# Ranks between the two halves of the turn of x's rows, and the rows' transfers behind the ranks

## The chip, the cores and the metric

The kernel runs on one core of a Trainium2 chip. A core has five engines with instruction streams of their own: TensorE (PE in the profile, its weight loads PEld), VectorE (DVE), ScalarE (ACT), GpSimd (POOL) and SyncE (SP), which here only issues DMA transfers. They meet at semaphores. The metric is the device time of one execution in microseconds, as the median of several runs.

## The reference

A retention layer (linear attention with a decay per head) and, on its output, a mixture of experts with one expert for each token. B = 4 sequences of S = 768 tokens, H = 8 heads of D = 64, so 3072 tokens of 512 numbers; 8 experts with a hidden layer of 1024.

```python
# retention, for every head h with its decay gamma[h]
for t in range(S):
    state = gamma * state + outer(k[:, :, t], v[:, :, t])
    y[:, :, t] = scale * q[:, :, t] @ state
x = y.transpose(0, 2, 1, 3).reshape(B * S, H * D)
# the mixture: each token goes to the expert of its highest logit
xn = x / (norm(x) + 1e-6)
en = expert_emb / (norm(expert_emb) + 1e-6)
probs = softmax(xn @ en.T / tau)
e = argmax(probs, axis=1)
out = probs[e] * (relu(x @ w1[e]) @ w2[e])
```

## The kernel before

**Stages.** The retention runs first, then the eight experts, with some overlap at the seam. The retention is cut into blocks of 256 tokens, NM = 12 in all, three to a sequence. Its output, x, is written to a scratch tensor in DRAM (`xd`). Each token is given a slot in a table (`tbl`), sorted by expert, and the experts then gather their tokens' rows of x through that table. Expert 0 starts early, on the 288 of its slots that are filled first.

**Order.** The whole order is written out by hand: within an engine, instructions run in the order in which the program issues them, and the same holds for the transfers that SyncE issues. So where a line stands in the loop decides what waits behind it.

**One iteration m of the retention loop** (L754 to L882). `scores` makes 32 products of k and q into four PSUM banks (L374), and `masks` multiplies them on VectorE with the causal mask (L394), two banks for each half u of the block. `inter` (L444) adds the part of the carried state, and `state` (L408) makes the next block's. `logits_products` (L481) makes the router's logits of block m-1, `logits_rows` turns them on VectorE (L489). Then k and q of block m+1 are transposed (L343, L361) and copied by ScalarE. At the end of the iteration `intra` (L449) multiplies masked scores with v, and `take` (L451) copies the block's output from PSUM to `yTs[m]`.

**Rows of x.** `yTs[m]` has features on the partitions, and `xd` wants tokens as rows. `rows_turn(m)` (L458) turns the block with two VectorE transposes in blocks of 32 by 32, one for each half u of 128 tokens, from `yTs[m]` into a tile `x`. `rows(m)` (L465) then issues four transfers of that tile to `xd` on SyncE (L468). It is called for block m-1 near the end of iteration m (L853), ahead of `intra`. Three buffers hold `yTs`, two hold `x`.

**Slots.** The blocks are routed in groups: GROUPS = (0,1,2), (3,4,5), (6,7), (8), (9,10), (11). In the iteration after the last block of a group (`done`, L756), `sums` and `choose` pick each token's expert, and `add_counts` adds the group to the running counts. At the start of the next iteration (`waiting`, L757) `count` makes the ranks' sums on TensorE (L526 to L530), and `ranks` computes from them on VectorE rank and slot of each token (three instructions, `rs` L546, `rank` L548, `sloti` L550). `place` (L559) writes tokens into the table with indirect transfers on GpSimd, two to four for an iteration. `done` is set at m = 3, 6, 8, 9 and 11, so the ranks are computed at the start of m = 4, 7, 9 and 10; at m = 11 they come in the same iteration, in another branch.

**PSUM banks.** `pt_` hands out four banks (b0 to b3) in turn. In an iteration that starts with ranks, the first bank goes to the counts, the next four requests to the scores, then come the logits and the transposes. So the second half of the scores needs the bank that `rs` has read, and the logits and the transposes need banks that the masks have read.

**GpSimd.** `scale_k` and `scale_q` (L337, L332) of block m+2 wait for the first mask of iteration m; behind them stand the table writes of that iteration.

**The seam to the experts.** At the end of m = 8 two pieces of expert 0's weights are loaded (`load_piece`, L881, eight transfers at L191). At m = 9 and 10 `early_slots` reads table entries back on SyncE (L597), and at m = 10 `early_gather` fetches their rows from `xd` on GpSimd (L588, three transfers into `xge`). Two more pieces are loaded between the slot reads of m = 10. The rows of block 9 are written behind the last early gather (`gathered`). At m = 11 TensorE transposes `xge` (L607).

Of the kernel before, what the change touches and what calls it, by code (L numbers as in the profile page):

```python
# [11 lines left out]
F32 = mybir.dt.float32  # L12
# [12 lines left out]
P = 128  # L25
# [3 lines left out]
NM = B * NCB  # L29
# [5 lines left out]
KT = DM // P  # L35
FT = DF // P
Q = 32
NQ = P // Q
# [66 lines left out]
def retention_moe(ctx: ExitStack, tc: tile.TileContext, q, k, v, emb, tau, w1, w2, const, const16, out):  # L105
# [52 lines left out]
    def pt_():  # L158
        npt[0] += 1
        return bank(turn_of[npt[0] % len(turn_of)])  # L160
# [12 lines left out]
    def after(i, o):  # L173
        tc.add_manual_dep(i.ins, o.ins.name, SYNC, reason="pace")
# [135 lines left out]
    ap_ = ctxa.enter_context(tc.tile_pool(name="ap", bufs=2))  # L310
# [14 lines left out]
    def load_v(m, h=slice(0, H)):  # L325
        return load(vin[m % 4], v, m, h)
# [23 lines left out]
    def transpose_k(m, s, copy=nc.scalar.copy):  # L350
        ps = pt_()
        turn_k(m, s, ps)
        return copy_k(m, s, ps, copy)
# [43 lines left out]
    def state(m):  # L397

        if m % NCB == 0:
            for u in range(2):  # L400
                pst[u] = bank(f"pst{u}").rearrange("p (j c) -> p j c", j=KT)
        for j in range(KT):
            for sk in range(2):
                for u in range(1 + (m % NCB < NCB - 1)):
                    for a in range(2):
                        r = slice(u * 64, (u + 1) * 64)
                        h = 2 * j + a
                        i = nc.tensor.matmul(pst[u][a * D:(a + 1) * D, j, :D], ks_r[r, m % 3, sk, h, :], vin[m % 4][r, h, sk, :],  # L408
                                         start=(m % NCB == 0 and j == 0 and sk == 0), stop=True, skip_group_check=True)
        return i  # L410

    def state_copy(m):
        if m % NCB < NCB - 1:
            tBs[m] = ap_.tile([P, KT, D], F32, name="tB")
            nc.scalar.copy(out=tBs[m], in_=pst[1][:, :, :D])

    def state_sums(m):

        s1 = Ss[m, 1] = ap_.tile([P, KT, D], F32, name="s1")
        if m % NCB:  # L420
            nc.vector.tensor_tensor(out=s1, in0=pst[0][:, :, :D], in1=tBs[m - 1], op=ALU.add)
        else:
            nc.vector.tensor_copy(out=s1, in_=pst[0][:, :, :D])
        if m % NCB < NCB - 1:
            s0 = Ss[m + 1, 0] = ap_.tile([P, KT, D], F32, name="s0")
            nc.vector.tensor_tensor(out=s0, in0=pst[0][:, :, :D], in1=tBs[m], op=ALU.add)
# [3 lines left out]
    def py_of(m):  # L430
        pys[m] = [bank(f"py{u}").rearrange("p (j c) -> p j c", j=KT) for u in range(2)]
# [14 lines left out]
    def intra(m, u):  # L446
        for j in range(KT):
            for a in range(2):
                y_product(m, u, j, a, vs[m][:, u, 2 * j + a], pms[a, u][:, j])  # L449
# [5 lines left out]

            nc.scalar.copy(out=yTs[m][o * D:(o + 1) * D, :, P:], in_=pys[m][1][(1 - o) * D:(2 - o) * D])

    def rows_turn(m):  # L458
        x = ap_.tile([P, 2 * NQ, KT, Q], F32, name="x")
        for u in range(2):  # L460
            nc.vector.transpose(out=x[:, u * NQ:(u + 1) * NQ].rearrange("p g j a -> p j g a"),
                                in_=yTs[m][:, :, u * P:(u + 1) * P].rearrange("p j (g b) -> p j g b", b=Q))
        return x

    def rows(m, behind=None, x=None):  # L465
        x = rows_turn(m) if x is None else x
        for i in range(NQ):
            o = nc.sync.dma_start(  # L468
                out=xd[m * T2:(m + 1) * T2, i * P:(i + 1) * P].rearrange("(b g) x -> b g x", b=Q),
                in_=x[i * Q:(i + 1) * Q].rearrange("b g j a -> b g (j a)"))  # L470
            if behind is not None:
                after(o, behind)
# [19 lines left out]
    def span(g):  # L492
        return slice(2 * GROUPS[g][0], 2 * GROUPS[g][-1] + 2)
# [28 lines left out]
    def count(g):  # L522
        r = span(g)
        nb = r.stop - r.start
        pr = pt_()
        nc.tensor.matmul(pr[:, :nb * NE], ones, cum[:, r.start:r.start + 1].broadcast_to([P, nb, NE]), start=True,  # L526
                         stop=False, skip_group_check=True)
        nc.tensor.matmul(pr[:, :nb * NE], tri, oh[:, r], start=False, stop=False, skip_group_check=True)
        for i in range(1, nb):
            nc.tensor.matmul(pr[:, i * NE:nb * NE], ones, oh[:, r.start:r.stop - i], start=False, stop=(i == nb - 1),  # L530
                             skip_group_check=True)
        return pr
# [9 lines left out]
    def ranks(g, pr):  # L542
        r = span(g)
        nb = r.stop - r.start
        rs = ap_.tile([P, nb, NE], F32, name="rs", bufs=1)
        nc.vector.tensor_tensor(out=rs, in0=pr[:, :nb * NE].rearrange("p (c e) -> p c e", e=NE), in1=oh[:, r], op=ALU.mult)  # L546
        yield
        nc.vector.tensor_reduce(out=rank[:, r], in_=rs, axis=AX.X, op=ALU.add)  # L548
        yield
        nc.vector.scalar_tensor_tensor(out=sloti[:, r], in0=wmn[:, r], scalar=16.0 * STRIDE, in1=rank[:, r],  # L550
                                       op0=ALU.mult, op1=ALU.add)
        yield
# [13 lines left out]
    def run_all(*gs):  # L566
        gs = list(gs)
        while gs:
            gs = [g for g in gs if next(g, gs) is not gs]
# [29 lines left out]
    def early_gather(j):  # L599
        n = EROWS[j][1]  # L600
        indices(n, 0, slice(j, j + 1))
        return gather(xge, n, j, 0, j, SEALS[j] * P)
# [151 lines left out]
    for m in range(NM):  # L754
        nxt = m + 1 < NM
        done = last_of.get(m - 1)  # L756
        if waiting is not None:  # L757
            run_all(ranks(waiting, count(waiting)))
            ready += range(span(waiting).start, span(waiting).stop)
        py_of(m)  # L760

# [26 lines left out]
        if m == NM - 2:  # L788
# [5 lines left out]
            gathered = early_gather(2)  # L794
# [7 lines left out]
        if m == 0:  # L802
            state(0)
            state_copy(0)
            state_sums(0)
            intra(0, 0)
            intra(0, 1)
            transpose_k(1, 0)
            i = transpose_k(1, 1)
            after(load_v(2), i)  # L810
            inter(0)
            transpose_q(1, 0)
            i = transpose_q(1, 1)
            for j in (*load_q(3), load_k(3), load_v(3)):
                after(j, i)
            state(1)
            state_copy(1)
            state_sums(1)
        else:
            inter(m)  # L820
            if nxt:
                i = state(m + 1)
                state_copy(m + 1)
                if m + 3 < NM:
                    after(load_k(m + 3), i)
            if m == 2:
                after(nc.sync.dma_start(
                    out=tbl.rearrange("(e s) c -> e (s c)", e=NE)[:, :FILL * SW].rearrange("e (p x) -> e p x", p=P // NE),
                    in_=none), i)
            for i in () if m < 3 else (0, 1, 2) if m == 3 else (m - 1,):  # L830
                logits_rows(i, logits_products(i))
            if m == NM - 5:
                pad(0)
            if m == NM - 3:
                pad(1)
            if not nxt:
                pad(2)
            if nxt:
                state_sums(m + 1)
                spread_v(m, 1, nc.vector.tensor_copy)  # L840
                transpose_k(m + 1, 0)
                transpose_q(m + 1, 0)
                i = transpose_q(m + 1, 1)
                if m + 3 < NM:
                    after(load_v(m + 3), i)
                transpose_k(m + 1, 1)
                if done is not None:
                    z = sums(done)
                    run_all(choose(done, z))
                    run_all(add_counts(done))  # L850
                if m == NM - 2:
                    lows[1]()
                rows(m - 1, gathered if m == NM - 2 else None)  # L853
                if m == NM - 2:
                    load_piece(gathered)
                    load_piece(gathered)
                intra(m, 0)
                intra(m, 1)
            else:
                intra(m, 0)  # L860
                z = sums(done)
                run_all(choose(done, z))
                run_all(add_counts(done))
                intra(m, 1)
                ps = [turn_rows(xge, EROWS, kt, bank(f"pst{kt}")) for kt in range(2)]
                pr = count(done)
                run_all(ranks(done, pr))
                place(range(span(done).start, span(done).stop))
# [37 lines left out]
    m, g = NM - 1, len(GROUPS) - 1  # L906
# [12 lines left out]
    x = rows_turn(m - 1)  # L919
# [251 lines left out]
    for e in range(1, NE):  # L1171
# [36 lines left out]
        done, pend = pend, None  # L1208
# [123 lines left out]
```

## Time and profile before

| | us |
|---|---|
| median of 3 runs | 414.15 |
| lowest and highest run | 413.32, 414.84 |
| the profiled execution's own time | 416.23 |
| its span, first to last instruction | 414.5 |
| mean granted TensorE clock in it | 0.983 |

The profile is one execution. Its page gives busy time for each engine, the span in 40 slices, and the chain of work that ended last. A timeline row has the start in us from the start of the span, the length in us, engine, line, operation, output and inputs, shapes and how many instructions are merged; in brackets stands the idle time before it and what ended that. A row of windows has, for a stretch of the span, its length, and busy time and number of instructions for PE, PEld, DVE, ACT and POOL, then granted clock, share of the DMA engines' time, and GB/s. Ends of matmuls are modelled, and a wait is put down to the semaphore that came last.

### The profile page before, as it was taken

Reading aid. Unit: us, or ns where it says so; the run is one execution under the profiler, and the core shown is the slowest. Engines: PE = TensorE matmul, PEld = TensorE weight load, DVE = VectorE, ACT = ScalarE, POOL = GpSimd, SP = SyncE. Lnnn points to the kernel's source line nnn. Section 1 sums busy time; section 2 is a strip of 40 time slices with the busy share of each in tenths; the row PEclk is TensorE's granted clock in tenths of the full one; section 3 lists DMA queues with packets and bytes.
Section 4 is the critical chain, followed back from the end, with each engine's and each line's share of the span. In section 5 each row is a group of like instructions: output and inputs, shape, how many; then the busy total and the mean of one; then the engine's idle time right before and its main releaser. Section 6 shows DMA issues by size and latency. Waiting matters only on the chain.

```text
span 414.5 us, 9548 instructions
## 1 busy us (share of the span) xinstructions
PE 400.9 (97%) x3648; PEld 367.0 (89%) x3648; DVE 255.0 (62%) x538; ACT 214.3 (52%) x381; POOL 157.4 (38%) x178
## 2 busy tenths in 40 slices
PE   7999999998999999999999999999999999999993
PEld 4898888886878988999899999999999889989982
DVE  5597868776668848651972865747567546745400
ACT  4565666554473435752753736724745655545210
POOL 2766566767815430521711521520331281011011
PEclk9999999999599999999999999999999999999997
DMA  8898898875653779488688797776977978631001
GB/s 251 266 311 244 253 281 241 247 208 151 167 157 83 237 291 284 115 262 259 204 278 210 268 323 186 254 252 213 262 244 242 272 266 288 187 153 74 1 26 51
DMA packets 88575, 88.67 MB, mean 214 GB/s; under 512 B 10604, under 2 KB 67052, under 8 KB 88520
## 3 DMA queue, kind: packets, MB, share of 16 engines
q1 hardware_dynamic: 83416, 74.79, 60.1%
q0 software_dynamic: 4928, 13.11, 8.9%
q8 instruction: 30, 0.49, 0.5%
q14 instruction: 25, 0.20, 0.2%
q10 hardware_dynamic: 176, 0.07, 0.1%
HBM read 65.14 MB, written 19.04 MB: 203 GB/s over the span
## 4 chain that ended last, share of the span: by engine, by line
PE 73%; issue 9%; DMA 5%; DVE 5%; ACT 3%; POOL 2%; SPq 1%; POOLq 0%; DVEq 0%; ACTq 0%
PE pst L1020 9%; PE py L237 9%; PE b L237 9%; PE py L437 8%; PE pst L237 6%; PE b L374 6%; PE py L1062 4%; PE pst L1062 4%; PE b L1020 4%; PE py L1020 3%; PE pst L408 3%; PE b L343 3%; PE b L361 2%; DMA xg<-xs 2%; PE b L481 2%
## 5 line engine op out<-in xcount | busy, mean ns | idle before, releaser
L222 DVE TENSOR_TENSOR wlo<-raw,whi 128x1024 fp32r<-128x1024 f32 x64 | 77.8, 1217 | 29.1 <-ACT whi L216 23.8
L1044 POOL DMA_INDIRECT out_dram<-og,si x29 | 29.1, 1002 | 141.9 <-ACT og L1037 105.1
L216 ACT CAST whi<-raw 128x1024 fp32r<-128x1024 f32 x64 | 66.2, 1043 | 2.5 <-DMA raw<-in_moe_w_dram 2.4
L588 POOL DMA_INDIRECT xr<-xd,gi x26 | 32.5, 1250 | 24.3 <-ACT sq L271 16.5
L394 DVE TENSOR_TENSOR pm<-b,mask 128x512 f32<-128x512 f32 x48 | 29.7, 681 | 9.6 <-PE b L374 9.6
L337 POOL TENSOR_TENSOR hl<-wlo,cst 128x512 f32<-128x512 f32 x22 | 22.5, 1041 | 31.1 <-DMA wlo<-in_k_dram 15.0
L237 PE MATMUL b<-xh,wlo 128*128 128x384 f32 (+5 forms) x96 | 32.4, 338 | 0.7 <-DVE wlo L222 0.7
L237 PE MATMUL b<-xl,whi 128*128 128x384 f32 (+5 forms) x96 | 32.6, 340 | 0.0
L237 PE MATMUL b<-xh,whi 128*128 128x384 f32 (+5 forms) x96 | 32.5, 339 | 0.0
L559 POOL DMA_INDIRECT tbl<-zt,sloti x24 | 25.0, 1041 | 17.1 <-DVE sloti L550 11.3
L237 PE MATMUL py<-xl,whi 128*128 128x384 f32 (+5 forms) x92 | 31.5, 343 | 0.0
L374 PE MATMUL b<-qT,kT 64*128 64x128 f32 x384 | 27.5, 281 | 2.9 <-issue 1.0
L1003 DVE STREAM_TRANSPOSE xt<-xg 128x416 f32<-128x416 f32 (+1 forms) x28 | 15.8, 582 | 23.2 <-DMA xg<-xs 23.1
L237 PE MATMUL py<-xh,whi 128*128 128x384 f32 (+5 forms) x88 | 29.7, 338 | 0.0
L237 PE MATMUL py<-xh,wlo 128*128 128x384 f32 (+5 forms) x88 | 29.5, 335 | 0.0
L1020 PE MATMUL pst<-hh,whi 128*128 128x288 f32 (+4 forms) x88 | 29.3, 333 | 0.0
L1020 PE MATMUL pst<-hl,whi 128*128 128x288 f32 (+4 forms) x88 | 29.2, 332 | 0.0
L1020 PE MATMUL pst<-hh,wlo 128*128 128x288 f32 (+4 forms) x88 | 29.1, 331 | 0.0
L374 PEld LDWEIGHTS b<-qT,kT 64*128 64x128 f32 x384 | 23.8, 187 | 5.6 <-issue 2.2
L243 ACT ACTIVATE hh<-b 128x384 fp32r<-128x384 f32 (+5 forms) x24 | 11.8, 490 | 30.0 <-PE b L237 30.0
L243 ACT ACTIVATE hh<-py 128x384 fp32r<-128x384 f32 (+5 forms) x23 | 11.0, 483 | 27.2 <-PE py L237 24.7
L437 PE MATMUL py<-pm,vs 128*64 128x128 f32 x384 | 24.8, 280 | 0.1
(223 smaller groups left out, 1033.5 us busy)
## 6 DMA issues: line engine op xcount, KB each, us to landing
raw<-in_moe_w_dram SPq DMA_DIRECT2D x60, 512.0 KB
whi<-in_q_dram SPq DMA_DIRECT2D x24, 256.0 KB
xd<-x SPq DMA_DIRECT2D x48, 128.0 KB
wlo<-in_k_dram SPq DMA_DIRECT2D x11, 512.0 KB
xs<-xr SPq DMA_DIRECT2D x6, 768.0 KB
xg<-xs SPq DMA_DIRECT2D x16, 208.0 KB
whi<-in_v_dram SPq DMA_DIRECT2D x6, 512.0 KB
wlo<-in_v_dram SPq DMA_DIRECT2D x6, 512.0 KB
```

Of the source, the lines that this page charges most:

```text
L216: nc.scalar.copy(out=views[1], in_=views[0])
L222: nc.vector.tensor_tensor(out=views[2], in0=views[0], in1=views[1].bitcast(F32), op=ALU.subtract)
L237: nc.tensor.matmul(acc[:, :w], a[:, f], x[:, kt, cols], start=(kt + i == 0), stop=(kt == KT - 1 and i == len(terms) - 1))
L243: nc.scalar.activation(out=hh[:, ft, cols], in_=acc[:, :w], func=AF.Relu)
L374: nc.tensor.matmul(psc[a][:, j], kTs[m][a * D:(a + 1) * D, j, u].rearrange("p s c -> p (s c)"), q_cols(m, a, j, u), start=True, stop=True, ...
L394: o.append(nc.vector.tensor_tensor(out=pm, in0=psc[a], in1=w, op=ALU.mult))
L437: nc.tensor.matmul(pys[m][u][o * D:(o + 1) * D, j], lhsT, rhs, start=first, stop=True, skip_group_check=True)
L559: i = nc.gpsimd.indirect_dma_start(out=tbl[:, :], out_offset=bass.IndirectOffsetOnAxis(ap=sloti[:, n:n + 1], axis=0), in_=zt[:, n], in_off ...
L588: return nc.gpsimd.indirect_dma_start(out=xr[:n, j, :], out_offset=None, in_=xd[:rows_, :], in_offset=bass.IndirectOffsetOnAxis(ap=gi[:n, ...
L1020: nc.tensor.matmul(acc[:, :c], a[:, f], x[:, kt, :c], start=(n == 0), stop=(n == 3 * FT - 1))
L1044: i = nc.gpsimd.indirect_dma_start(out=out[:, :], out_offset=bass.IndirectOffsetOnAxis(ap=si[:n, e, j:j + 1], axis=0), in_=og[:n, j, :], i ...
L1062: nc.tensor.matmul(acc[:s, :], x[:, kt, at], a, start=(n == 0), stop=(n == 3 * FT - 1))
```

## The change

Where a group is complete (`done` is set, m = 3, 6, 8, 9), `rows_turn` turns only the first half of block m-1, and no rows are transferred in that iteration. The second half and the four transfers come in the next iteration, behind the ranks and ahead of the scores and masks. In the other iterations nothing changes. The table writes, the masks and everything else keep their places relative to the ranks.

```diff
-    def rows_turn(m):
-        x = ap_.tile([P, 2 * NQ, KT, Q], F32, name="x")
-        for u in range(2):
+    def rows_turn(m, us=range(2), x=None):
+        if x is None:
+            x = ap_.tile([P, 2 * NQ, KT, Q], F32, name="x")
+        for u in us:
             nc.vector.transpose(out=x[:, u * NQ:(u + 1) * NQ].rearrange("p g j a -> p j g a"),
                                 in_=yTs[m][:, :, u * P:(u + 1) * P].rearrange("p j (g b) -> p j g b", b=Q))
         return x
...
         if waiting is not None:
             run_all(ranks(waiting, count(waiting)))
+            rows(m - 2, x=rows_turn(m - 2, (1,), x))
             ready += range(span(waiting).start, span(waiting).stop)
         py_of(m)
...
-                rows(m - 1, gathered if m == NM - 2 else None)
+                if done is not None:
+
+                    x = rows_turn(m - 1, (0,))
+                else:
+                    rows(m - 1, gathered if m == NM - 2 else None)
```

On SyncE the four transfers of block 2 and of block 5 move behind nothing else; those of block 7 move behind the eight weight transfers at the end of m = 8 and stand ahead of the first slot read of m = 9; those of block 8 stand ahead of the second slot read of m = 10.

## The prediction

> **What bounds the kernel now.** I read the page first, for the busy shares and the granted clock, then the windows around the place where the clock falls, then the timelines of VectorE, TensorE, GpSimd and the DMA queue from 40 to 125 us, where all edited lines run.
>
> ```profile
> PE 400.9 (97%) x3648; PEld 367.0 (89%) x3648; DVE 255.0 (62%) x538; ACT 214.3 (52%) x381; POOL 157.4 (38%) x178
> PEclk9999999999599999999999999999999999999997
> ...
> 89.40:92.80 3.40, 3.21 (x54) 2.70 (x57) 2.30 (x8) 2.92 (x5) 1.05 (x3) 1.00 0.74 198
> 99.70:103.10 3.40, 2.07 (x23) 1.53 (x23) 1.54 (x6) 1.69 (x4) 1.29 (x2) 1.00 0.41 103
> 103.10:113.40 10.30, 9.95 (x101) 8.19 (x101) 7.37 (x12) 5.64 (x8) 8.75 (x12) 0.50 0.64 174
> ```
>
> TensorE is the bound: it is busy for 400.9 of 414.5 us, VectorE for 62% only. So an edit on VectorE and the DMA queue moves the time only where TensorE waits for them. The window rows (length, PE, PEld, DVE, ACT, POOL, clock, DMA share, GB/s) show the one weak place: TensorE is busy 2.07 of 3.40 us, and right after it runs 10.3 us at half clock.
>
> The change touches four places. In each, VectorE turns the rows (two transposes), then computes ranks, then masks:
>
> ```profile
> L461 DVE STREAM_TRANSPOSE x<-yT x24: 668/680/712, 23.7 to 132.4; 128x512 f32<-128x512 f32 x24
> ...
> 43.74 1.30 DVE L461 STREAM_TRANSPOSE x<-yT 128x512 f32<-128x512 f32 x2
> 44.97 0.17 DVE L546 TENSOR_TENSOR rs<-b,oh 128x48 f32<-128x48 f32 x1
> 45.49 0.69 DVE L394 TENSOR_TENSOR pm<-b,mask 128x512 f32<-128x512 f32 x1
> ...
> 69.44 1.31 DVE L461 STREAM_TRANSPOSE x<-yT 128x512 f32<-128x512 f32 x2
> 70.67 0.17 DVE L546 TENSOR_TENSOR rs<-b,oh 128x48 f32<-128x48 f32 x1
> 71.20 0.68 DVE L394 TENSOR_TENSOR pm<-b,mask 128x512 f32<-128x512 f32 x1
> ...
> 88.11 1.30 DVE L461 STREAM_TRANSPOSE x<-yT 128x512 f32<-128x512 f32 x2
> 90.44 0.19 DVE L546 TENSOR_TENSOR rs<-b,oh 128x32 f32<-128x32 f32 x1 [1.03 <-PE b L374]
> 90.97 0.68 DVE L394 TENSOR_TENSOR pm<-b,mask 128x512 f32<-128x512 f32 x1
> ...
> 98.85 1.30 DVE L461 STREAM_TRANSPOSE x<-yT 128x512 f32<-128x512 f32 x2
> 101.94 0.17 DVE L546 TENSOR_TENSOR rs<-b,oh 128x16 f32<-128x16 f32 x1 [1.79 <-PE b L374]
> 102.43 0.68 DVE L394 TENSOR_TENSOR pm<-b,mask 128x512 f32<-128x512 f32 x1
> ```
>
> The reader is to see two kinds of place. At 44 and 70 us the ranks start as soon as the second transpose is over, so that transpose is what they wait for. At 90 and 102 us VectorE has been idle for 1.03 and 1.79 us, and TensorE ends the wait.
>
> **The change part by part.** Nothing is removed or added: 4 of the 24 transposes (680 ns each; a pair takes 1.30, so a half costs about 0.65 us) and 16 of the 48 row transfers move.
>
> *Ranks ahead of the half turn.* At 44 and 70 us the ranks come up to 0.6 us sooner, at 90 and 102 us not at all. What would use the sooner ranks is TensorE, through the PSUM bank of the counts, which the ranks free, and the table writes on GpSimd.
>
> ```profile
> 44.10 2.25 PE L374 MATMUL b<-qT,kT 64*128 64x128 f32 x32
> 70.00 2.09 PE L374 MATMUL b<-qT,kT 64*128 64x128 f32 x32 [0.18 <-issue]
> 102.17 1.22 PE L374 MATMUL b<-qT,kT 64*128 64x128 f32 x14 [0.82 <-DVE rs L546]
> ```
>
> At 44 and 70 us the 32 score products run through without waiting for the ranks. The one wait, 0.82 us at 102.17, is where the ranks themselves wait for TensorE and do not come sooner. Gain taken: 0. Bounds: no loss, since the ranks never come later; at most 0.65 us, if that wait were all VectorE's.
>
> *The half turn ahead of the masks.* At 44 us the order changes and the sum does not, so the masks stay at 45.5; at 70 us they move by 0 to 0.3. At 90 and 102 us the transposes leave an idle stretch and go where VectorE was working: masks 0.65 us later each. The cover is what TensorE does before it needs the banks that the masks free:
>
> ```profile
> 93.73 0.64 PE L481 MATMUL b<-yT,enT 128*32 128x256 f32 x8
> 94.34 0.63 PE L343 MATMUL b<-ident,hl 128*128 128x128 f32 x4
> ...
> 94.44 0.45 DVE L489 STREAM_TRANSPOSE parts<-b 128x256 f32<-128x256 f32 x1 [0.99 <-PE b L481]
> 109.01 0.45 DVE L489 STREAM_TRANSPOSE parts<-b 128x256 f32<-128x256 f32 x1 [2.35 <-PE b L481]
> ```
>
> The four masks from 90.97 end at about 93.5 and would end at 94.1. The logits at 93.73 take the bank of the first mask, free at 92.3; the transposes at 94.34 take that of the third, free at about 93.5. VectorE then idles 0.99 and 2.35 us waiting for TensorE: 0.65 fits into both. Cost taken: 0. With the cover gone it is 2 x 0.65 = 1.3 us.
>
> *GpSimd.* The scaling of k and q waits for the first mask, so it starts 0.65 us later in one iteration, and the four table writes behind it too:
>
> ```profile
> 91.80 2.04 POOL L337 TENSOR_TENSOR hl<-wlo,cst 128x512 f32<-128x512 f32 x2 [2.35 <-PE b L374]
> 108.24 1.10 POOL L588 DMA_INDIRECT xge<-xd,gi  x1 [0.27 <-POOL gi L582]
> 111.46 1.71 POOL L588 DMA_INDIRECT xge<-xd,gi  x1 [0.37 <-POOL gi L582]
> ```
>
> Its k and q serve the next iteration, over 8 us on. Cost 0.
>
> *The transfers, and the DMA queue behind them.* The queue issues in program order, and a transfer that waits holds all behind it.
>
> ```profile
> 86.74 0.37 SPq L315 DMA_DIRECT2D wlo<-in_v_dram  x1
> 89.44 2.57 SPq L468 DMA_DIRECT2D xd<-x  x4
> 92.06 4.86 SPq L191 DMA_DIRECT2D raw<-in_moe_w_dram  x8
> ...
> 100.18 2.55 SPq L468 DMA_DIRECT2D xd<-x  x4
> 102.83 0.55 SPq L597 DMA_DIRECT2D tb<-tbl  x1
> 103.42 2.91 SPq L191 DMA_DIRECT2D raw<-in_moe_w_dram  x4
> 107.55 0.31 SPq L597 DMA_DIRECT2D tb<-tbl  x1
> 107.90 1.84 SPq L191 DMA_DIRECT2D raw<-in_moe_w_dram  x4
> 114.80 3.38 SPq L468 DMA_DIRECT2D xd<-x  x4
> ...
> 117.38 1.99 ACT L216 CAST whi<-raw 128x1024 fp32r<-128x1024 f32 x2
> 120.74 1.16 PE L607 MATMUL pst<-ident,xge 128*128 128x128 f32 x6
> ```
>
> In the first two places the four issues start about 0.5 us later, and behind them stand loads that are used iterations later (three iterations lie between 43.74 and 69.44, so 8.6 us each). In the third place the 8 weight pieces, which wait for nothing, go first: from about 87.2 instead of 92.06, and the rows from 92.1 instead of 89.44. Their megabyte then meets the loads of k and v, but queues behind them. In the fourth place the half turn ends at 103.1, and 2.55 us of row transfers now stand ahead of the slot reads: 102.83 becomes about 105.8, the pieces 103.42 become 106.4, the second slot read 107.55 about 109.5. Next late is the third early gather, 111.46: between 111.46 (its slots come in time) and 114.4 (the whole 2.9 us), and I take 112.8, as 107.55 has waited for a part of this already. Its landing releases the next row transfers, 114.80 before, 116.1 then. Its reader on TensorE is at 120.74, its cover thus 120.74 - 114.80 = 5.9 us against 1.3 to 2.9. The later pieces would be issued by about 112; their casts at 117.38 leave over 5 us, and the four issues before needed 1.84. Cost taken: 0. If the cover were gone, up to 2.9 us.
>
> **Sum**: 0 + 0 + 0 + 0 = 0 against the profiled execution's 416.23 us (span 414.5 and 1.7 around it), so also 0 against the median of 414.15, which lies 0.5% below it. Bounds without the clock: -0.65 to +1.3 + 2.9 = +4.2 us, the upper end only with all covers gone, against rows that show each of them.
>
> **The rivals.** *The half-clock stretch goes (faster).* The row 99.70:103.10 has TensorE busy 61% of the window, the row 89.40:92.80 has 94%, and no drop follows it. So the drop hangs on some 1.3 us of idle time, 0.82 of it in the wait for the ranks, and the change moves what GpSimd and the DMA queue do in these microseconds: the weight pieces are through earlier, the four table writes come 0.65 us later, no rows are issued at 100.18. If that fills the window, 9.95 us of products at half clock take half: 5.0 us less. The third early gather's reader would then stand at 115.8, against a landing at 116.1, so some 0.3 comes back: 414.15 - 4.7 = 409.5. For it: one window, once. Against it: the ranks wait for TensorE there, and nothing in the change lets TensorE signal sooner.
> [...]
>
> *A second drop (slower).* The masks at 90 us come 0.65 us later. If TensorE then waited for their banks at 93.7 to 95 us and the next window fell as low as the one at 99.7, another 10.3 us at half clock would cost 5.0 us: 419.2. It decides where a window falls from 94% busy to about 61%, that is 1.1 us more of idle. The delay of 0.65 alone does not reach this, and VectorE's 0.99 us of slack speaks against it.
>
> *Covers partly gone.* The 1.3 us of masks show, and no more: 415.5, within the measurement.
>
> **How the numbers follow.** No change, 0.58, with 412.1 to 416.2 as its own range; the drop goes, 0.24; something slower, 0.18, two thirds of it the second drop or the slot chain late beyond its cover (+2.9: 417.0). A difference below 0.5%, about 2.1 us, can hardly be told from none here; the runs shown already spread from 413.32 to 414.84. Forecast 414.2. The range goes from 409.2, which takes in the faster rival, to 417.0, and leaves out the second drop and what lies beyond. Faster 0.24, same 0.58, slower 0.18.
>
> **What would show it.** In the changed kernel's timelines: in the first two places one transpose of about 0.68 us stands between cum and rs and one between sloti and the masks, with the masks within 0.3 us of where they were; in the last two the ranks still wait for TensorE, the idle time before rs grows by about 0.65, and the masks follow that much later. The first weight pieces are issued before the rows, at about 87 us, and the first slot read of the next iteration comes about 3 us later. TensorE's logits and the transposes of the early rows wait for none of it. I am wrong if the granted clock has no half-speed stretch near 103 us or has two, or if the products of the early rows wait for their gather.

## The result, and the profile after

The changed kernel took 419.5 us (median of 20 runs, 414.03 to 424.88), the kernel before 415.18 (20 runs, 413.09 to 422.84). The ratio is 1.0064, 95% interval 1.0038 to 1.0089: the change costs about 2.7 us. The ratio leaves out runs more than 1.5% above the fastest of their kernel, eight of the changed kernel's 20 and one of the 20 before, so it is smaller than that of the two medians. The forecast was 414.2 with a range to 417.0, so the result lies above the range. The profiled execution of the changed kernel took 419.04 us, its span is 417.3.

First the page of the changed kernel, and two windows of its trace (length, then busy time and instructions of PE, PEld, DVE, ACT and POOL, then granted clock, DMA share, GB/s).

```profile
PE 401.8 (96%) x3648; PEld 367.9 (88%) x3648; DVE 259.5 (62%) x538; ACT 214.5 (51%) x381; POOL 159.3 (38%) x178
...
PEclk9999999999599999999999999999999999999997
```

```profile
102.50:105.90 3.40, 0.74 (x12) 0.74 (x13) 0.90 (x4) 2.34 (x4) 1.28 (x3) 1.00 0.02 5
105.90:116.10 10.20, 10.20 (x104) 8.58 (x103) 8.19 (x13) 4.47 (x7) 7.79 (x9) 0.50 0.71 193
```

TensorE does the same 3648 products in nearly the same busy time (401.8 us, 400.9 before), and in this execution there is still one stretch at half clock, of the same length (10.20 us, 10.30 before). What has grown is the hole in front of it: TensorE is busy for 0.74 of 3.40 us, where it was 2.07. The list of TensorE's waits from 30 to 125 us (us in all, times, longest) names it:

```profile
PE b L374 <- DVE rs L547: 3.1, 2, 2.9
PE py L437 <- DVE vs L387: 1.2, 3, 0.6
```

The longest wait for the ranks was 0.82 us before; it is 2.9 now. Now rows of the changed kernel's timeline, from all engines in order of time; `remote` in brackets means that the view found the semaphore that ended the wait and no instruction to put it down to.

```profile
72.86 1.25 DVE L394 TENSOR_TENSOR pm<-b,mask 128x512 f32<-128x512 f32 x2
...
72.96 3.95 SPq L469 DMA_DIRECT2D xd<-x  x4
78.35 0.54 SPq L315 DMA_DIRECT2D wlo<-in_k_dram  x1
85.32 2.04 POOL L337 TENSOR_TENSOR hl<-wlo,cst 128x512 f32<-128x512 f32 x2 [3.89 <-DMA wlo<-in_k_dram]
88.94 6.25 SPq L191 DMA_DIRECT2D raw<-in_moe_w_dram  x8
...
94.07 2.48 DVE L394 TENSOR_TENSOR pm<-b,mask 128x512 f32<-128x512 f32 x4 [0.32 <-PE b L374]
94.90 2.04 POOL L337 TENSOR_TENSOR hl<-wlo,cst 128x512 f32<-128x512 f32 x2 [1.62 <-DVE pm L394]
96.90 2.04 POOL L332 TENSOR_TENSOR hh<-whi,cst 128x512 f32<-128x512 f32 x2
99.10 1.01 POOL L560 DMA_INDIRECT tbl<-zt,sloti  x1 [0.15 <-issue]
100.81 0.17 PE L531 MATMUL b<-oh,ones 128*128 128x8 f16 x1
...
102.98 0.98 POOL L560 DMA_INDIRECT tbl<-zt,sloti  x1 [0.30 <-issue]
104.93 0.17 DVE L547 TENSOR_TENSOR rs<-b,oh 128x16 f32<-128x16 f32 x1 [3.10 <-remote]
105.42 0.71 DVE L462 STREAM_TRANSPOSE x<-yT 128x512 f32<-128x512 f32 x1
106.05 2.45 DVE L394 TENSOR_TENSOR pm<-b,mask 128x512 f32<-128x512 f32 x4
106.15 3.15 SPq L469 DMA_DIRECT2D xd<-x  x4
109.40 0.56 SPq L598 DMA_DIRECT2D tb<-tbl  x1
```

And the rows of the kernel before that answer to them:

```profile
70.78 2.57 SPq L468 DMA_DIRECT2D xd<-x  x4
75.63 0.54 SPq L315 DMA_DIRECT2D wlo<-in_k_dram  x1
...
81.56 2.04 POOL L337 TENSOR_TENSOR hl<-wlo,cst 128x512 f32<-128x512 f32 x2 [1.76 <-DVE pm L394]
...
98.54 0.17 PE L530 MATMUL b<-oh,ones 128*128 128x8 f16 x1
99.96 0.98 POOL L559 DMA_INDIRECT tbl<-zt,sloti  x1 [0.31 <-issue]
```

Read from the ranks backwards. The counts that `rs` needs are the three small products; the last of them starts at 98.54 before and 100.81 after, 0.17 us long. Yet `rs` starts at 101.94 (quoted in the prediction) and 104.93, over 3 us behind them. What it does follow is GpSimd: the last table write ends at 99.96 + 0.98 = 100.94 before and 103.96 after, and `rs` starts 1.00 and 0.97 us later. So in these two traces VectorE goes on about 1 us behind the end of the last table write, and not when the counts are ready. The traces show the times; how GpSimd's writes could hold back what TensorE signals, they do not show. Nor is it always the last write: ScalarE's copy of the block's output (L456) starts in the changed kernel at 103.51, 2.7 us behind the products it reads (99.72 to 100.81) and 0.83 us behind the end of the third of the four writes, in the middle of the fourth. If the writes are what holds the counts, there is a closed chain: the first mask of an iteration releases the scaling (94.07 to 94.90), the scaling takes 4.0 us (94.90 to 98.94), then come four table writes, 1.29 us apart (99.10 to 102.98), then about 1 us until TensorE's result is seen, then the ranks, and behind them, now, the half turn, and then the next first mask (106.05). The ranks of m = 10 stand 3.0 us later than before; the span is 2.8 us longer.

Not all of the 3.0 us is the change. These are VectorE's copies of v ahead of the first moved instruction, in the kernel before and in the changed one, and the changed kernel's first half turn and its masks of m = 4:

```profile
41.07 0.97 DVE L387 COPY vs<-wlo 64x512 f32<-64x512 f32 x2
...
40.99 2.32 DVE L387 COPY vs<-wlo 64x512 f32<-64x512 f32 x2
45.00 0.71 DVE L462 STREAM_TRANSPOSE x<-yT 128x512 f32<-128x512 f32 x1
46.78 2.44 DVE L394 TENSOR_TENSOR pm<-b,mask 128x512 f32<-128x512 f32 x4
```

The copies took 1.35 us longer in this execution, so the first half turn starts at 45.00 where the turn before started at 43.74. The masks of m = 4 stand as far behind it as before (1.78 and 1.75 us), as the prediction had it, and are late only for that reason. From first mask to first mask, the way from m = 4 to 7 takes 25.7 us before and 26.1 after, from 7 to 9 19.8 and 21.2, from 9 to 10 11.5 and 12.0. So the largest step lies between m = 7 and 9, where the next row stands.

That row is 85.32. There the scaling waits 3.89 us for its load of k, issued at 78.35 behind row transfers that now run from 72.96 to 76.91; before, the load was issued at 75.63, and at 81.56 the mask released the scaling. Whether the change brings this wait about is open: in `before_act_copy` below, whose rows stand where they stood before, the scaling of the same iteration waits 3.19 us for its k (85.54), and in the second run of the change, `after_again`, the mask releases it (83.05).

### The profile page after: what moved, and what is told of

Its sections match the earlier page's. It is cut to its first block, busy times and chain, and to the rows that moved or that the text cites. A ratio compares the mean times of both kernels' runs of the same rounds, so it can differ in the third digit from the quotient of the medians.

```text
span 417.3 us, 9550 instructions
## 1 busy us (share of the span) xinstructions
PE 401.8 (96%) x3648; PEld 367.9 (88%) x3648; DVE 259.5 (62%) x538; ACT 214.5 (51%) x381; POOL 159.3 (38%) x178
## 4 chain that ended last, share of the span: by engine, by line
PE 80%; issue 7%; DVE 6%; DMA 2%; another core or an unknown queue 1%; POOL 1%; ACT 1%; SPq 1%; POOLq 0%; DVEq 0%
PE pst L1026 11%; PE b L237 11%; PE py L237 11%; PE pst L237 8%; PE py L437 6%; PE b L1026 5%; PE b L374 4%; PE py L1026 4%; PE py L1068 4%; PE pst L1068 4%; PE pst L408 2%; PE b L343 2%; PE b L361 2%; DVE vs L387 2%; PE b L1068 1%
## 5 line engine op out<-in xcount | busy, mean ns | idle before, releaser
L337 POOL TENSOR_TENSOR hl<-wlo,cst 128x512 f32<-128x512 f32 x22 | 22.7, 1054 | 33.3 <-DMA wlo<-in_k_dram 19.8
L1010 ACT CAST xh<-xt 128x384 fp32r<-128x384 f32 (+4 forms) x28 | 14.4, 519 | 20.9 <-DVE xt L1009 20.9
```

Of the source, the lines that this page charges most:

```text
L337: return eng.tensor_tensor(out=ks_r[:, m % 3, s, h], in0=kin[m % 3][:, h, s], in1=w[:, h], op=ALU.mult)
```

## The experiments

There were six sets of runs, each on one chip with runs of the kernel before beside it. They fall into two kinds: in four the kernel before took 415.2 to 416.2 us, in two 409.3 to 410.0. In profiles of the first kind `rs` of m = 10 starts about 1 us behind the end of GpSimd's last table write (1.00 us in the kernel before, 0.97 in the changed one, 1.16 in `change_third`; in `both_halves_third` the masks are held instead, shown below). In `both_halves`, `both_halves_again` and `change_paired`, of the second kind, `rs` of m = 10 has no idle time in front of it. I call them **held** and **free** sets; sets 2 and 3 stand with the held ones by the time of the kernel before.

| set, kind, before (us) | kernel | ratio to before, 95% interval |
|---|---|---|
| 1, held, 415.18 | the change | 1.0064 [1.0038, 1.0089] |
| 2, held, 416.01 | after_again (the change) | 1.0051 [1.0016, 1.0085] |
| | transfers_only | 1.0022 [0.9993, 1.0051] |
| | transfers_behind_loads | 1.0059 [1.0025, 1.0094] |
| | behind_masks | 1.0109 [1.0067, 1.0151] |
| 3, held, 416.17 | first_two | 1.0028 [0.9992, 1.0063] |
| | last_two | 1.0040 [1.0006, 1.0074] |
| | before_act_copy | 0.9998 [0.9964, 1.0033] |
| | after_act_copy | 1.0044 [1.0012, 1.0075] |
| 4, free, 409.99 | last_two_behind_masks | 1.0065 [1.0036, 1.0094] |
| | both_halves | 1.0004 [0.9975, 1.0033] |
| | before_writes_first | 1.0267 [1.0234, 1.0300] |
| | after_writes_first | 1.0206 [1.0164, 1.0247] |
| 5, free, 409.32 | change_paired (the change) | 1.0033 [0.9996, 1.0070] |
| | both_halves_again | 1.0031 [0.9996, 1.0065] |
| | before_no_pace | 1.0042 [1.0014, 1.0069] |
| | after_no_pace | 1.0046 [1.0009, 1.0082] |
| 6, held, 416.24 | change_third (the change) | 1.0042 [1.0019, 1.0066] |
| | both_halves_third | 1.0103 [1.0063, 1.0143] |

### Which part: the order of the turn or the transfers

**The change again.** 

> The changed kernel once more, as the measure for its siblings: 2 to 4 us above the kernel before under every theory. Its profile should again have GpSimd's scaling waiting for a load of k late in the retention, and vs copies on VectorE of about 1.2 us in place of 0.42.

Measured 1.0051: the loss is there in a second set. The wait for a load of k late in the retention, which was expected again, is not in this profile (83.05, above).

**The transfers alone.** Both halves are turned at the old place, only the transfers stand behind the ranks.

```diff
-            rows(m - 2, x=rows_turn(m - 2, (1,), x))
+            rows(m - 2, x=x)
...
-                    x = rows_turn(m - 1, (0,))
+                    x = rows_turn(m - 1)
```

> Both halves are turned at the old place, only the row transfers come behind the ranks. Theory queue (the transfers now stand directly ahead of the loads of q, k and v on the DMA queue, k comes late, GpSimd scales late and collides with VectorE's vs copies): as slow as the change, +2 to +4 us. Theory masks (the half turn ahead of the masks delays the first mask, and GpSimd with it): within 1 us of the kernel before.

Measured 1.0022, with 1 inside the interval. It tells little: at m = 4 and 7 the tile is ready and nothing stands between the two places in the queue, so the transfers hardly move there.

**The transfers behind the loads.** The change, but at m = 4 and 7 the four transfers stand behind that iteration's loads of q, k and v.

```diff
-            rows(m - 2, x=rows_turn(m - 2, (1,), x))
+            rows_turn(m - 2, (1,), x)
+            if m + 3 >= NM:
+                rows(m - 2, x=x)
...
+                if waiting is not None and m + 3 < NM:
+                    rows(m - 2, x=x)
```

> As the change, but at m = 4 and 7 the row transfers stand behind the loads of q, k and v of that iteration. Theory queue: at least two thirds of the loss goes, within 1 us of the kernel before. Theory masks: as slow as the change, +2 to +4 us.

Measured 1.0059: the loss stays. GpSimd's timeline of this kernel shows what released the scaling in three iterations:

```profile
63.36 2.04 POOL L337 TENSOR_TENSOR hl<-wlo,cst 128x512 f32<-128x512 f32 x2 [2.52 <-DVE pm L394]
72.66 2.04 POOL L337 TENSOR_TENSOR hl<-wlo,cst 128x512 f32<-128x512 f32 x2 [2.79 <-DVE pm L394]
...
93.16 2.05 POOL L337 TENSOR_TENSOR hl<-wlo,cst 128x512 f32<-128x512 f32 x2 [2.85 <-DVE pm L394]
```

It waits for the first mask, as before the change, and not for the load of k. In these iterations no load is late, and the loss is there.

**Everything behind the masks.** The half turn and the transfers stand behind the four masks.

```diff
-            rows(m - 2, x=rows_turn(m - 2, (1,), x))
...
+        if waiting is not None:
+            rows(m - 2, x=rows_turn(m - 2, (1,), x))
```

> As the change, but the second half turn and the transfers come behind the four masks, still ahead of the loads. Theory queue: slower than the change, by 0 to 3 us, as the loads behind the transfers come another 2.4 us later. Theory masks: within 1 us of the kernel before, as the first mask is 0.65 us sooner than there.

Measured 1.0109, against at most 1 us by the theory of the masks: by the chain through the first mask it should have been nearly free, with the half turn off that way. GpSimd's timeline shows a possible reason:

```profile
59.01 2.22 POOL L337 TENSOR_TENSOR hl<-wlo,cst 128x512 f32<-128x512 f32 x2 [4.24 <-DMA wlo<-in_k_dram]
67.77 2.04 POOL L337 TENSOR_TENSOR hl<-wlo,cst 128x512 f32<-128x512 f32 x2 [1.90 <-DMA wlo<-in_k_dram]
```

Here the transfers start later still, the loads of k behind them too, and the scaling waits for the load. So there may be two ways into the same chain, by the mask and by the load of k. That the late load is what costs here was not tested: the half turn now also stands ahead of everything that VectorE does behind the masks, and no run separates the two.

**Two places each.** `done is not None and m < 7` keeps the change at m = 3 and 6 alone, `and m > 7` at m = 8 and 9 alone.

> The change at m = 3 and 6 alone (blocks 2 and 5). Theory queue (at m = 4 and 7 the transfers of two blocks and the loads of a third meet on the DMA queue, k comes late): carries nearly the whole loss, +2 to +3 us. Theory path (the half turn of 0.65 us now lies between TensorE's counts and VectorE's masks, which was idle waiting for TensorE only at m = 9 and 10): within 0.5 us of the kernel before.

> The change at m = 8 and 9 alone (blocks 7 and 8). No q, k or v is loaded behind these transfers. Theory queue: within 0.5 us of the kernel before. Theory path: +1.3 to +3 us.

Measured 1.0028 and 1.0040, together 0.68%, about the 0.42 to 0.64% of the whole. Each has an interval of some 0.35% to either side, and that of the first takes in 1, so the runs fit a loss that is spread over the places, and do not show it.

### A rival: VectorE's copies beside GpSimd's scaling

In the first profile of the change VectorE's copies of v (L387) came to lie beside GpSimd's scaling and took up to 1.30 us each where the shortest take 0.42, and TensorE waited 1.2 us for them in all (the list of waits above). The trace shows the longer copies beside the scaling (2.32 us for the two from 40.99, with the scaling of q from 40.79 to 43.02); what passes between the two engines it does not show. In these two kernels ScalarE makes the second copy instead:

```diff
-                spread_v(m, 1, nc.vector.tensor_copy)
+                spread_v(m, 1)
```

> The kernel before, with the second half of v's spread copied by ScalarE and not VectorE, so that no copy on VectorE can meet GpSimd's scaling. Theory port (the loss is made by VectorE's copies of 0.42 us, which take up to 1.2 us beside GpSimd's scaling): the spread of the runs gets smaller; the median may go either way by 2 us, as ScalarE has 1.24 us more for an iteration.

> The changed kernel with the same copies on ScalarE. Theory port: within 1 us of before_act_copy, as the change can no longer make the copies collide. If the loss does not pass through the copies: 2 to 3 us above before_act_copy.

Measured 0.9998 for the kernel before with this edit and 1.0044 for the changed one: between the two stands about the same loss as without the edit, so nothing here makes the collision its main cause. The intervals, some 0.33% to either side, leave room for a part. That it can cost much is shown by the next pair, in which the table writes stand ahead of the scaling:

```diff
+        if m == NM - 3:
+            early_slots(0)
+        place(ready[:n])
+        del ready[:n]
...
-        if m == NM - 3:
-            early_slots(0)
-        place(ready[:n])
-        del ready[:n]
```

> The kernel before, with GpSimd's table writes ahead of its scaling, so that they are over before the end of the iteration. Theory loop: the chain is cut, TensorE's signal behind the second intra product follows it within 0.1 us where it took up to 3.3 us, and the time falls by 2 to 8 us (8 if the half clock stretch near 103 us goes too). If the writes have no part in it: within 1 us of the kernel before.

> The changed kernel with the same order on GpSimd. Theory loop: the half turn is off the closed chain, so the difference to before_writes_first falls to 1 us or less. Theory path: it stays at 2 to 3 us.

Measured 1.0267 and 1.0206. The scaling is pushed onto the copies; in the kernel before with this edit:

```profile
103.85 4.89 DVE L387 COPY vs<-wlo 64x512 f32<-64x512 f32 x2
103.95 2.07 POOL L337 TENSOR_TENSOR hl<-wlo,cst 128x512 f32<-128x512 f32 x2
105.95 2.05 POOL L332 TENSOR_TENSOR hh<-whi,cst 128x512 f32<-128x512 f32 x2
```

Two copies that take 0.84 us alone last 4.89 and end only behind the scaling (108.0). Why they last that long, the trace does not show. This collision makes the pair useless as a test of the chain: the kernel before with this edit was 11 us slower, where 2 to 8 us of gain were expected if the writes hold the ranks.

### The dose, in both kinds of set

**Both halves behind the ranks.** VectorE now has 1.3 us of transposes instead of 0.65 between ranks and masks, at all four places:

```diff
-            rows(m - 2, x=rows_turn(m - 2, (1,), x))
+            rows(m - 2)
...
-                    x = rows_turn(m - 1, (0,))
+                    x = None
```

> Both halves of the turn behind the ranks, ahead of the masks, at all four places: twice the dose. Theory loop: about twice the loss of the change, +4 to +5 us. Theory of a late transfer alone: as the change, +2 to +3 us, as the transfers hardly come later.

Set 4 is free: 1.0004, at most 0.33% by the interval. Twice the dose costs nothing that can be measured. In the same set the last two places alone, with the half turn behind the masks:

> As last_two, but the second half turn and the transfers come behind the four masks. Theory loop (first mask, GpSimd's scaling, its table writes, TensorE's signal for the counts about 1 us behind the last write, ranks, first mask again: a closed chain, in which the half turn stands): the chain is free of the half turn, so 0 to 0.5 us above the kernel before, against about 1.7 us of last_two. Theory path (any VectorE work behind the ranks costs): as slow as last_two.

Measured 1.0065, 2.7 us, where the chain theory had 0 to 0.5; with its interval it can be as slow as `last_two` (1.0040), as the other theory had it. Its list of TensorE's waits from 100 to 125 us shows other waits than the change has:

```profile
PE pst L608 <- DMA xge<-xd,gi: 1.6, 2, 1.2
PE py L437 <- POOL vs L387: 1.6, 1, 1.6
```

Ahead of the early rows no half-clock stretch shows here (the logits at 109.14 take 0.64 us; at 110.42 in the changed kernel's first profile, at a clock of 0.50, they take 1.08), TensorE comes to them at 113.72 (at 123.41 in the changed kernel's first profile), and the late slot reads and gathers are no longer covered. So the rival of the late slot chain shows where TensorE is early, and it does not explain the held sets: the changed kernel's list of waits above has no such row.

The change itself was still to be compared with its double in one set.

> The changed kernel once more, as the base for the three others on the same chip. Chain theory (first mask, GpSimd's scaling, the table writes, TensorE's signal about 1 us behind the last write, the ranks): where the ranks come about 1 us behind the last write of the iteration before, +1.3 to +2.7 us over the kernel before; where TensorE's signal follows its last product at once, 0 to +0.5. Late slot reads: +1.2 to +2.9 on either, with a wait of TensorE for the gathered rows at about 114 to 121 us in the profile.

> Both halves of the turn behind the ranks in all four places, so twice the VectorE time ahead of the masks; the transfers start about 0.65 us later than in the change. Chain theory: where the ranks come about 1 us behind the last table write, twice the loss of the change (+4 to +5 us over the kernel before); where they do not, 0 to +1. Late slot reads: the loss of the change plus at most 0.65 us.

This set was free too: 1.0033 and 1.0031, both with 1 inside the interval, and no step from the one dose to the other. The other pair of this set takes the first mask out of the chain, so that the scaling waits for its data alone:

```diff
-                after(scale_k(m + 2, s), i)
+                scale_k(m + 2, s)
...
-                after(scale_q(m + 2, s), i)
+                scale_q(m + 2, s)
```

> The kernel before, where GpSimd's scaling of k and q waits for its data alone and no longer for the first mask. Chain theory: faster than the kernel before by 0 to 2 us, since the scaling and the table writes behind it start sooner, if the ranks are not themselves late; a collision of the scaling with VectorE's turn or copies could take this back. It is the base for the next run, not a verdict by itself.

> The change, with the scaling no longer waiting for the first mask, to be compared with the run before it. Chain theory: with the step from the first mask to the scaling cut, the half turn ahead of the masks holds nothing on GpSimd, so 0 to +0.8 us over the kernel before without that wait. Late slot reads, or masks that TensorE waits for directly: the same +2 to +2.7 us as with the wait.

Measured 1.0042 and 1.0046: the kernel before becomes slower by it, where 0 to 2 us of gain were expected, and there is no loss from one to the other that can be measured. In a free set the chain theory expects little loss to begin with, so this cut was not tested where it matters.

The last pair fell on a held set.

> The changed kernel, beside the next run on the same chip. Chain theory: +2 to +2.7 us over the kernel before if the profile shows the ranks about 1 us behind the last table write (the kernel before then takes about 416); 0 to +1 if TensorE's results are signalled at once (the kernel before then takes about 410). Late transfers and slot reads: about +1.4 in both cases.

> Both halves of the turn behind the ranks in all four places: twice the VectorE time ahead of the masks, transfers 0.65 us later than in the change. Chain theory: +4 to +5 us over the kernel before where the ranks come about 1 us behind the last table write, 0 to +1 where they do not. Late transfers and slot reads: as the change, at most 0.65 us more.

Measured 1.0042 and 1.0103. In us, on 416.24: +1.7 and +4.3, which is the doubling and more. In set 5, which is free, the same step from the one dose to the other was nothing. This pair is the best evidence for a cost of VectorE's work between ranks and masks in a held set. It doesn't say by which way that cost goes: the transfers start 0.65 us later too. The traces of the doubled kernel in both kinds show the difference. First the held one (rows of all engines):

```profile
76.16 2.44 DVE L394 TENSOR_TENSOR pm<-b,mask 128x512 f32<-128x512 f32 x4
83.75 0.98 POOL L560 DMA_INDIRECT tbl<-zt,sloti  x1 [0.30 <-issue]
85.69 2.48 DVE L394 TENSOR_TENSOR pm<-b,mask 128x512 f32<-128x512 f32 x4 [2.65 <-PE b L374]
...
102.94 1.38 PE L374 MATMUL b<-qT,kT 64*128 64x128 f32 x18
...
106.30 0.98 POOL L560 DMA_INDIRECT tbl<-zt,sloti  x1 [0.30 <-issue]
107.58 0.98 POOL L560 DMA_INDIRECT tbl<-zt,sloti  x1 [0.30 <-issue]
108.24 0.45 PE L437 MATMUL py<-qT,s 64*64 64x128 f32 x3 [1.11 <-issue]
109.16 1.14 POOL L589 DMA_INDIRECT xge<-xd,gi  x1 [0.28 <-issue]
109.67 0.58 PE L437 MATMUL py<-qT,s 64*64 64x128 f32 x3 [0.98 <-issue]
111.10 1.24 PE L437 MATMUL py<-qT,s 64*64 64x128 f32 x17 [0.85 <-issue]
111.16 1.29 DVE L394 TENSOR_TENSOR pm<-b,mask 128x512 f32<-128x512 f32 x2 [4.56 <-remote]
```

At 85.69 the masks start 0.96 us behind the last write (83.75 + 0.98 = 84.73). At 111.16 they start 0.86 us behind the gather that ends at 110.30, after 4.56 us of waiting for score products whose records begin at 102.94. And TensorE itself moves in steps: its products go on at 108.24, 109.67 and 111.10, each 0.8 to 1.1 us behind the end of one of GpSimd's indirect transfers (107.28, 108.56, 110.30). Now the same kernel in the free set (set 5):

```profile
74.26 2.44 DVE L394 TENSOR_TENSOR pm<-b,mask 128x512 f32<-128x512 f32 x4
...
99.70 0.17 PE L531 MATMUL b<-oh,ones 128*128 128x8 f16 x1
99.76 0.98 POOL L560 DMA_INDIRECT tbl<-zt,sloti  x1 [0.30 <-issue]
99.92 0.17 DVE L547 TENSOR_TENSOR rs<-b,oh 128x16 f32<-128x16 f32 x1
101.04 0.98 POOL L560 DMA_INDIRECT tbl<-zt,sloti  x1 [0.31 <-issue]
101.73 2.45 DVE L394 TENSOR_TENSOR pm<-b,mask 128x512 f32<-128x512 f32 x4
```

Here `rs` starts 0.05 us behind the counts (99.87), in the middle of a write, and the masks do not wait either. From the first mask of m = 7 to that of m = 10 the doubled kernel takes 27.5 us free (74.26 to 101.73) and 35.0 held (76.16 to 111.16; half clock, which shows on its page as 0.6 in the slice from 105.0 to 115.4, can have a part in this). The change itself, with half the dose, takes 28.5 in the same free set (74.14 to 102.68), so there the dose adds nothing to this stretch. The changed kernel and the one before, held, take 33.2 (72.86 to 106.05) and 31.2 (71.20 to 102.43).

**The clock in the ratios.** A ratio is taken over many executions, and each of them has its own mean granted clock. Averaged over the executions behind the ratios, the clock of the held sets is lower with the change: 0.9877 against 0.9913 for the kernel before in set 2, 0.9878 against 0.9905 in set 6, and 0.9857 for `after_act_copy` against 0.9883 for `before_act_copy`. In set 5, which is free, it is 0.9936 for both. A mean clock that is lower by 0.003 over 416 us is, as an estimate, up to 1.2 us, if TensorE is busy throughout. That makes up to 1.5 of 2.1 us in set 2 and 1.1 of 1.7 in set 6. Only in set 2 is the difference of the clocks clear of the scatter between executions, and for set 1 the clocks of the kernel before are known for its profiled execution only. So a large part of the loss in held sets may be more time at half clock. Whether the deeper hole brings that time about, or both only vary together, no run shows. The step from the change to its double shows little of it: the clocks are 0.9878 and 0.9872, by the same estimate 0.2 us of the 2.6, though with wide scatter.

## Why the prediction was wrong

**The failed step**, as far as the runs show it, is the term "GpSimd": "Its k and q serve the next iteration, over 8 us on. Cost 0." I asked only who needs the scaled k and q, and not what stands behind the scaling on its engine, though I had named the four table writes, and not who goes on when those end. In the profiles of held sets above the ranks or masks of the next iteration go on 0.86 to 1.16 us behind a write or gather. The 1.79 us of waiting before `rs` at 101.94 was in the prediction as "TensorE ends the wait"; the records of TensorE's counts end at 98.71, 3.2 us sooner, so the wait names an engine whose counts had long been made. What the runs put in place of the sum of 0: +1.7 to +2.7 us for the change in the held sets (1.0042 to 1.0064), about +4.3 for its double, and no measurable step between the two where the results are not held. These are prices of the whole change. How much of them goes through the table writes, how much through the load of k and how much is half clock was not measured, so the cause is argued from times and from the doubled dose. The edge from mask to scaling was not cut in a held set, and behind_masks, which takes the half turn off it in one, lost more (1.0109).

**Ranks ahead of the half turn:** gain 0 was right. The ranks of the last two places still wait, and nothing came sooner. The idle time before `rs` was to grow by about 0.65 us at both; it grew at m = 10 (1.79 to 3.10) and shrank at m = 9 (1.03 to 0.40).

**Half turn ahead of the masks:** the delay was right where I looked for it. At m = 10 the masks start 0.63 us behind the start of the second transpose (105.42 to 106.05). The cover I named, TensorE's banks and VectorE's idle time before the logits, was too narrow: the first mask also releases GpSimd.

**Transfers and queue:** "loads that are used iterations later" was false. The load of k issued at 75.63 feeds the scaling at 81.56, in the next iteration, and issued 2.7 us later it decided the start of the scaling in this execution (85.32). That is a second possible way into the chain. The order held and the times did not: the weight pieces went first, from 88.94 (forecast 87.2), the rows behind them at 95.47 (forecast 92.1), and the slot read stands at 109.40, 6.6 us later than before where about 3 was forecast. It is still 3.25 us behind the start of the row transfers; what came on top is that those start late. TensorE did not wait for the early rows in the changed kernel's first profile; in last_two_behind_masks, without the half clock, it did, for 1.6 us.

**The rivals:** in the profiled execution the half-clock stretch neither went nor came twice, and the early rows did not wait, so none of the signs by which the prediction was to know itself wrong appeared. The time of 419.2 given for a second drop was near the result by luck, as far as this execution goes. The slot chain (+2.9) is near the loss in size, but its wait is not in this trace. None of the rivals was the chain through GpSimd.

**The clock:** the window before the half clock was 61% busy before and 22% (0.74 of 3.40) after, and the stretch behind it is 10.3 and 10.20 us long. In this pair the deeper hole did not make it longer. Other executions differ, as the mean clocks above show, so one pair does not clear the clock.

**What stays open.** Whether TensorE's products themselves or only the news of them are held back: the ends of matmul records are modelled, so the traces do not tell the two apart. Why the held sets show this and the free ones do not; one of each kind ran on a chip of the same number, so the chip may not be all of it. How the loss divides between mask, load of k and half clock. And whether the change costs about 0.3% in free sets too: one interval there runs from 0.9996 to 1.0070.

## What to carry to other kernels

When an edit delays an instruction, follow everything behind it on its engine, not only the reader of its output: here the likely price was that of the table writes queued behind a scaling whose own result had 8 us to spare. Where a wait names an engine, compare its end with that engine's own records: a gap like the 3.2 us here calls for another cause, and what ended shortly before on the other engines is the first to suspect. Before two profiles are compared late in the kernel, compare them ahead of the first moved instruction: 1.3 of the 3.0 us stood there. A small loss should be measured in more than one set of runs, with the kernel before beside it and with the granted clocks averaged, and here a doubled dose said more about its cause than halves did.

## What was not expected of the hardware

While GpSimd issued indirect transfers, in profiles of the held sets, instructions that read TensorE's results started about 1 us behind the end of one of these transfers, mostly the last (1.00, 0.97 and 0.86 us in the rows above), after waits of up to 4.56 us, and in `both_halves_third` TensorE's own products went on in steps with the transfers, 0.8 to 1.1 us behind their ends. In profiles of the free sets `rs` started 0.05 us (`both_halves_again`) and 0.08 us (`both_halves`) behind the counts, in the middle of a write. The kernel before is about 6 us slower on the first kind (415.2 to 416.2 against 409.3 to 410.0); that this comes from the held results was not tested by itself.
